# Another order of a forward attention segment, with V's turns taken off TensorE and a two-halves out-projection

## The chip, the core and the metric

The kernel runs on one core of one Trainium2 chip. The metric is the time of one execution on the device in microseconds: before the change 3229.96 us, the median of three runs from 3228.64 to 3230.3.

## What is computed

A transformer block with adaptive layer norms, forward and backward: an attention with a recurrent memory, then a gated feed-forward layer, then all gradients. The change is in the forward attention. Cut to that part, the reference is:

```python
mem = mem0                                  # 8 rows of 512
for s in range(64):                         # segments of 32 rows
    h = concat([mem, x[s * 32:(s + 1) * 32]])       # 40 rows
    q, k, v = h @ Wq, h @ Wk, h @ Wv                # 32 heads of 128
    p = softmax(where(mask, q @ k.T * scale, -1e9))
    o = (p @ v) @ Wo                                # over all heads: 40 rows of 512
    mem = o[:8]                                     # the next segment's memory
    outs.append(o[8:])
```

All inputs and outputs are bf16. The eight rows of memory make the segments strictly sequential: the projections of a segment need the first eight output rows of the one before.

## The kernel before, in words

`phase2` holds the forward attention: a Python loop over 64 segments that is unrolled into one instruction stream, in the order in which it is written. At its end the stream from the loop's start on is pinned (`pin`), so that each engine works through it in program order. Tiles have a fixed number of buffers; a write to a buffer waits for the reads of what it held.

**A and B rows.** Of the 40 rows of a segment, 8 are memory and 32 are input. The memory rows and the first 24 input rows are the 32 "A" rows, projected in the loop itself (`proj`, through `col_pass` at L222). The last eight input rows of four segments, 32 rows together, are projected in one "B" pass per Q, K and V ahead of time (`proj_b`). A pass is in two halves; each half is 16 matmuls of 512 columns, four of which lie side by side in four groups of 32 array columns, into one PSUM tile `pass_ps` [128, 512]. Partition group j holds rows 0 to 31 for a quarter of the heads. ScalarE or VectorE copies the half into row tiles `RA` or `RB`.

**The heads.** Eleven groups of three heads (the last of two) hold 120 rows each. For the first eight groups the three heads lie in partition groups 0 to 2; the heads of the last three groups come from partition group 3 of the row tiles, "far" pieces in what follows.

**Turning.** `turn_half` turns half a row tile by four TensorE transposes (L231); `to_heads` copies the result into `qT`, `kT` and `vT` (the tiles of `XT`), columns by group: one copy for the first eight groups, then one or two for the far ones. For A rows this is done in the loop for K, Q and V. For B rows a turned batch `b_cols` lies ready, from which GpSimd copies eight columns a head into the tiles (`tails_in`, L65).

**V in rows.** PV needs V in rows, `Vst` [128, 11 x 128]. GpSimd copies its first eight groups from `RA` (L715, L717), GpSimd-issued DMAs fill the tail rows 96 to 119 of these groups from `RBv` (`v_tails`, L624: three a segment), and the last three groups come back from `vT` by three TensorE transposes (`vst(2)`, L680).

**A segment**, in the order of its TensorE instructions:

1. the projections V, K, Q; meanwhile K and Q rows go to DRAM for the backward (`rows_out`, L554 and L555, issued by SyncE)
2. the turns: first halves of K and Q, both of V, second halves of K and Q; `vT` is stored whole to DRAM (L738)
3. `st_exp`: scores in three blocks of four, four and three groups, two matmuls a group (one adds the mask), then exp on ScalarE into `ET`
4. `den` and `pv` for each block: row sums by a matmul with ones, their reciprocal, PV into `or_ps`, and O scaled into `Ost` by one VectorE instruction (L694); SyncE issues a transposing DMA of `ET` into `Pst` (L748), for the backward
5. `ott`: O turned by TensorE transposes into `OT`; `Ost` and `OT` are stored (L771, L779)
6. `outproj`: 32 matmuls of 512 columns (`col_mm`, L211), one a head, four side by side, into `at_ps` [128, 512]; so four partial sums lie in four partition groups
7. `fold_split`: the partial sums as two bf16 parts each (hi by ScalarE, L278; the rest, lo, by VectorE, L282), in two halves of 256 columns
8. the slot "f2": a B pass of V, K or Q in the first three segments of four (both halves), the tail rows' out-projection in the fourth
9. `fold_sum`: eight matmuls (L291) with a selection matrix add the partial sums and turn the result; ScalarE copies its first eight columns into the next segment's `hT` (L785)

At the start of the next segment GpSimd normalizes the turned P of the last (`norm`, L792) and SyncE stores it (L794). GpSimd's order between two segments is: row store (L306), `v_tails`, `tails_in` for K, V and Q, `tail.collect` (L1822), the input part of `hT` (L511), the normalization, the two copies into `Vst`. In SyncE's: transpose of P, stores of O and O turned, B rows where there are any, store of P, K and Q rows.

In sixteen of the segments eight more matmuls and a weight load of the modulation (`mod_rest`) ride along, and a layer norm of later input rows (`p1`) is spread over each four segments.

The backward reads V turned once a segment, from the DRAM tile `VT`, as the moving operand of dO V (L1416).

Of the kernel before, what the change touches and what calls it, by code (L numbers as in the profile page):

```python
# [40 lines left out]
class K:  # L41
# [43 lines left out]
    def alloc_dram(self):  # L85
# [8 lines left out]
        self.VT = d("VT", [NS, 128, cfg.XW], BF16)  # L94
# [20 lines left out]
    def phase0(self):  # L115
# [10 lines left out]
        nc.vector.tensor_tensor(self.foldsel[:], fs2[:, 0, :], fs2[:, 1, :], op=ALU.add)  # L126
        self.later = []
# [80 lines left out]
    def col_mm(self, ps, lhsT, w, n, total):  # L208

        j = n % 4  # L210
        self.nc.tensor.matmul(ps[32 * j:32 * j + 32, :], lhsT=lhsT, rhs=w, start=(n < 4), stop=(n >= total - 4),  # L211
                              tile_position=(0, 32 * j))

# [190 lines left out]
    def phase2(self):  # L404
        nc, tc, cfg, io = self.nc, self.tc, self.cfg, self.io
        D, DC, H, E, L, M, T, G, NS = cfg.D, cfg.DC, cfg.H, cfg.E, cfg.L, cfg.M, cfg.T, cfg.G, cfg.NS
        GW = 128
# [10 lines left out]
        with ExitStack() as ctx:  # L418
# [26 lines left out]
            XT = {x: ptiles(x + "T", 1, w=cfg.XW)[0] for x in "qkv"}  # L445
# [26 lines left out]
            with tc.tile_pool(name="p0", bufs=1) as p0:  # L472
# [21 lines left out]
                for f in zeros:  # L494
                    f()
                self.load_heads(p0, Wv, io["A_Wv"])
                self.load_heads(p0, Wk, io["A_Wk"])
                p1(1, 0)
                self.load_heads(p0, Wq, io["A_Wq"])
# [38 lines left out]
            def to_heads(eng, xt, src, i0, n, r0, w, o):  # L538
# [4 lines left out]
                d = xt[:, 120 * i0:120 * (i0 + n)].rearrange("p (i x) -> p i x", x=120)[:, :, b:b + 3 * w]  # L543
                self.evac(eng, d.rearrange("p i (j r) -> p i j r", r=w), s4[:, :, 0:3, o:o + w])
# [23 lines left out]
            def b_pieces(t):  # L568
# [4 lines left out]
                def proj_b(x, hf):  # L573
                    hb = hxs[t][1]
                    pass_half(x, hf, lambda c: hb[:, c, :, :].rearrange("p s q -> p (s q)"), RBt[x], ("act", "dve")[hf])
                    if hf == 1 and x != "v":
                        rows_out(RBt[x], DR[x], t * nseg_t, nseg_t)

                def turn_b(x):
# [3 lines left out]
                    def f():  # L583
# [7 lines left out]
                return {(0, "f2"): [P("v", 0), P("v", 1)], (1, "f2"): [P("k", 0), P("k", 1)], (1, "turn"): [T_("v")],  # L591
                        (2, "f2"): [P("q", 0), P("q", 1)], (2, "turn"): [T_("k")], (3, "turn"): [T_("q")]}
# [8 lines left out]
            q_first = first.pop((2, "f2")) + first.pop((3, "turn")) + [evac_turned]  # L601
            for fs in first.values():
                for f in fs:
                    f()
            evac_turned()
# [8 lines left out]
            tail = TailRows(self, sb2, psp, psb, 1, "ao", self.AOB, 1)  # L614

            def tails_in(xs, s):
                for x in xs:
                    to_heads("pool", XT[x], btails[s // nseg_t][x][:], 0, 8, 32, 8, 8 * (s % nseg_t))

            def v_tails(s):  # L620

                for j in range(3):
                    o = 32 * j + 8 * (s % nseg_t)
                    nc.gpsimd.dma_start(Vst[96 + 8 * j:104 + 8 * j, 0:1024], RBv[(s // nseg_t) % 2][o:o + 8, 0:1024])  # L624

            v_tails(0)
            tails_in("vk", 0)
            i0 = len(self.traced())
            for s in range(NS):
# [6 lines left out]
                QT, KT, VT = XT["q"], XT["k"], XT["v"]  # L636
# [12 lines left out]
                def turn(x, hf, eng):  # L649
                    tp = turn_half(RA[x], hf)  # L650
                    to_heads(eng, XT[x], tp[:], 4 * hf, 4, 0, 32, 0)
# [13 lines left out]
                def den(pi):  # L665
# [7 lines left out]
                    nc.vector.reciprocal(rden[:, pi * PG:pi * PG + n], den_ps[0][0:120, pi * PG:pi * PG + n])  # L673
# [9 lines left out]
                def vst(pi):  # L683
                    ps, n = transposes_part(VT, pi, 120)
                    self.evac("act" if pi == 2 else "dve", part3(Vst, pi)[:, 0:n, :], ps)

                def pv(pi):
                    or_ps = ps_f32("or_ps")
                    n = min(PG, G - pi * PG)
                    for j in range(n):  # L690
                        g = pi * PG + j
                        nc.tensor.matmul(or_ps[:, j, :], lhsT=ET[:, g * GW:(g + 1) * GW], rhs=Vst[:, g * GW:(g + 1) * GW],  # L692
                                         start=True, stop=True)
                    nc.vector.tensor_tensor(part3(Ost, pi)[0:120, 0:n, :], or_ps[0:120, 0:n, :],  # L694
                                            rden[:, pi * PG:pi * PG + n].unsqueeze(2).to_broadcast([120, n, 128]), op=ALU.mult)

                def ott(pi):
                    ps, n = transposes_part(Ost, pi)
                    self.evac("dve" if pi == 2 else "act", part3(OT, pi)[:, 0:n, :], ps)

                at_ps = [None]
                n_at = [0]

                def outproj(h0, h1):
                    if at_ps[0] is None:
                        at_ps[0] = psp.tile([128, 512], F32, name="at_ps", tag="p")
                    for h in range(h0, h1):
                        off = (h // 3) * GW + (h % 3) * 32
                        self.col_mm(at_ps[0], OT[:, off:off + 32], Wo[:, h, :], n_at[0], H)
                        n_at[0] += 1  # L710
# [3 lines left out]
                proj("v", 0, "act")  # L714
                nc.gpsimd.tensor_copy(Vst[0:96, 0:512], RA["v"][0:96, 0:512])  # L715
                proj("v", 1, "dve")
                nc.gpsimd.tensor_copy(Vst[0:96, 512:1024], RA["v"][0:96, 512:1024])  # L717
                if s == NS - 1:
# [3 lines left out]
                if 1 <= s4 <= 3:  # L722
                    p1(s // nseg_t + P1_AHEAD, s4)
                proj("k", 0, "act")
                proj("k", 1, "dve")
                proj("q", 0, "dve")
                proj("q", 1, "act")
                if s == 0:
                    for f in q_first:
                        f()  # L730
                    tails_in("q", 0)
                turn("k", 0, "dve")
# [1222 lines left out]
```

## Time and profile before

| | |
|---|---|
| span of the profiled execution | 3233.1 us |
| TensorE (PE) busy | 2984.2 us, 92% |
| VectorE (DVE) busy | 1589.7 us, 49% |
| ScalarE (ACT) busy | 1200.4 us, 37% |
| GpSimd (POOL) busy | 1430.5 us, 44% |
| first and last copy into hT, 63 in all | 60.5 and 1042.3 us |
| transposing DMA of ET, time of its issue on SyncE | 1274 / 1407 / 2342 ns (least, median, most) |
| normalization of P on GpSimd | 2530 ns, 63 times |
| V tail DMA, issue on GpSimd | 511 ns median, 192 times |
| V tail DMA, issue to landing | 1.9 / 3.7 / 6.3 us |

How to read it: busy time counts an instruction from its start to its end, and matmuls overlap each other, so a high share of TensorE doesn't say by itself that it never waits. In timelines, the bracket at the end of a line gives the time in which the engine stood idle before it and what released it. "SPq" is the queue that SyncE issues DMAs from. PEld is the load of a stationary operand. Relative to the whole, the forward segments take about 1000 of 3230 us.

### The profile page before, as it was taken

What the parts mean: (1) busy time and instruction counts of PE and PEld (TensorE: products, weight loads), DVE (VectorE), ACT (ScalarE), POOL (GpSimd) and SP (SyncE); (2) the same over time, 40 slices, a digit from 0 to 9 for tenths busy, and PEclk for the clock granted to TensorE, in tenths of its full rate; (3) what the DMA queues carried; (4) which work ended last, traced back from release to release, by engine and by line L of the source; (5) the groups of instructions that cost most, each with busy time, mean ns of one, the idle gap of its engine ahead of it and who ended that gap; (6) DMA issues with size and microseconds to landing.
All of it is one profiled execution on the core that took longest, in us unless ns stands there. A gap on an engine that the chain in (4) does not pass through costs nothing.

```text
span 3233.1 us, 96019 instructions
## 1 busy us (share of the span) xinstructions
PE 2984.2 (92%) x38574; PEld 1709.9 (53%) x38650; DVE 1589.7 (49%) x4170; ACT 1200.4 (37%) x2842; POOL 1430.5 (44%) x3037
## 2 busy tenths in 40 slices
PE   6999999999998799988989999999999969999999
PEld 3555555555555444444555555555555534455454
DVE  5655555655555777642245545555554531322321
ACT  3555555555554333322134444444444420100111
POOL 3555555565555465630144444444444431333322
PEclk8999999999999899998999999999999989999999
DMA  8565555555555788896679999999999999898986
GB/s 295 174 173 169 171 169 172 165 172 173 162 164 174 220 212 210 211 260 217 219 199 263 265 247 273 261 261 259 258 272 258 261 233 219 241 209 198 202 231 159
DMA packets 862018, 699.40 MB, mean 216 GB/s; under 512 B 560690, under 2 KB 734274, under 8 KB 861444
## 3 DMA queue, kind: packets, MB, share of 16 engines
q1 hardware_dynamic: 737220, 483.44, 62.8%
q0 software_dynamic: 52912, 147.43, 13.4%
q10 hardware_dynamic: 71440, 62.40, 7.6%
q8 instruction: 304, 4.98, 0.7%
q14 instruction: 142, 1.16, 0.1%
HBM read 293.60 MB, written 275.02 MB: 176 GB/s over the span
## 4 chain that ended last, share of the span: by engine, by line
PE 43%; DMA 8%; ACT 2%; issue 2%; DVE 1%; SPq 1%; POOL 1%; ACTq 0%; DVEq 0%; POOLq 0%
PE dh_ps L211 9%; PE gps L1748 9%; PE pass_ps L222 4%; PE g_ps L1437 4%; PE gps L1146 3%; PE gps5o L1761 3%; PE dh_tps L211 2%; DMA rows<-DKR 2%; PE tps L1352 2%; PE dp_ps L1416 1%; DMA rows<-OSR 1%; PE dp_ps L1424 1%; ACT RAd L61 1%; PE dh_ft L291 1%; PE turn_ps L1318 1%
## 5 line engine op out<-in xcount | busy, mean ns | idle before, releaser
L1748 PE MATMUL gps<-rows,hrows 128*128 128x512 bf16 (+2 forms) x2124 | 415.8, 355 | 3.8 <-ACT ot L61 1.9
L1748 PEld LDWEIGHTS <-hrows 128*128 128x128 bf16 x2160 | 211.3, 98 | 206.6 <-issue 2.6
L222 PEld LDWEIGHTS <-hT 128*32 128x32 bf16 x6144 | 158.4, 97 | 177.9 <-ACT hT L785 24.5
L1466 POOL COPY dOst<-RAd 96x512 bf16<-96x512 bf16 x128 | 78.2, 612 | 355.9 <-DVE RAd L63 339.8
L1752 POOL DMA_DIRECT2D out_dram<-ot x108 | 81.2, 753 | 231.4 <-DVE ot L63 135.4
L63 DVE CAST ot<-gps 128x512 bf16<-128x512 f32 (+3 forms) x76 | 47.8, 632 | 247.8 <-DMA out_dram<-ot 99.1
L792 POOL TENSOR_TENSOR Pst<-Pst,rden 120x1408 bf16<-120x1408 bf16 x63 | 159.4, 2531 | 15.1 <-issue 7.1
L282 DVE TENSOR_TENSOR dh_lo<-dh_ps,dh_hi 128x256 bf16<-128x256 f32 x128 | 48.4, 420 | 239.1 <-ACT dh_hi L278 239.1
L1761 PE MATMUL gps5o<-WoT,rows 128*128 128x512 bf16 x588 | 131.6, 382 | 27.8 <-DMA rows<-OSR 27.2
L306 POOL DMA_DIRECT2D AOA<-at_rb x64 | 36.7, 574 | 250.8 <-DVE at_rb L305 137.3
L61 ACT ACTIVATE ot<-gps 128x512 bf16<-128x512 f32 (+3 forms) x75 | 41.0, 547 | 284.4 <-PE gps L1748 103.1
L222 PE MATMUL pass_ps<-Wv,hT 128*32 128x512 bf16 x2048 | 122.3, 380 | 18.1 <-ACT hT L785 18.1
L694 DVE TENSOR_TENSOR Ost<-or_ps,rden 120x512 bf16<-120x512 f32 (+1 forms) x192 | 124.3, 647 | 23.0 <-PE or_ps L692 0.8
L211 PE MATMUL dh_ps<-WvT,dVT 128*32 128x512 bf16 x2048 | 134.5, 381 | 0.2 <-issue 0.2
L1426 DVE SCALAR_TENSOR_TENSOR dS<-dp_ps,Pst_l 128x512 bf16<-128x512 f32 (+1 forms) x192 | 112.2, 640 | 35.3 <-PE dp_ps L1424 35.3
L222 PE MATMUL pass_ps<-WoT,dyT 128*32 128x512 bf16 x2048 | 121.9, 380 | 5.2 <-ACT dyT L1525 5.2
L211 PE MATMUL at_ps<-Wo,OT 128*32 128x512 bf16 x2048 | 123.3, 383 | 0.0
L211 PE MATMUL dh_ps<-WkT,dKT 128*32 128x512 bf16 x2048 | 122.6, 380 | 0.7 <-issue 0.7
L211 PE MATMUL dh_ps<-WqT,dQT 128*32 128x512 bf16 x2048 | 122.0, 379 | 0.0
L222 PE MATMUL pass_ps<-Wq,hT 128*32 128x512 bf16 x2048 | 121.6, 379 | 0.0
L222 PE MATMUL pass_ps<-Wk,hT 128*32 128x512 bf16 x2048 | 121.6, 379 | 0.0
L61 ACT ACTIVATE dVT<-g_ps 128x512 bf16<-128x512 f32 (+1 forms) x192 | 107.8, 562 | 35.9 <-PE g_ps L1437 20.0
(410 smaller groups left out, 7135.2 us busy)
## 6 DMA issues: line engine op xcount, KB each, us to landing
OSR<-Ost SPq DMA_DIRECT2D x64, 352.0 KB
OT<-OT SPq DMA_DIRECT2D x64, 352.0 KB
PS<-Pst SPq DMA_DIRECT2D x64, 352.0 KB
OT_l<-OT SPq DMA_DIRECT2D x64, 352.0 KB
Pst_l<-PS SPq DMA_DIRECT2D x64, 352.0 KB
DKR<-rows_x POOLq DMA_DIRECT2D x64, 352.0 KB, 6.0
DVR<-rows_x POOLq DMA_DIRECT2D x64, 352.0 KB, 7.5
DQR<-rows_x POOLq DMA_DIRECT2D x64, 352.0 KB, 6.1
```

The source lines that it names most:

```text
L61: return nc.scalar.activation(out, in_, AF.Copy)
L211: self.nc.tensor.matmul(ps[32 * j:32 * j + 32, :], lhsT=lhsT, rhs=w, start=(n < 4), stop=(n >= total - 4), tile_position=(0, 32 * j))
L222: self.nc.tensor.matmul(ps[32 * j:32 * j + 32, :], lhsT=lhs(c), rhs=rhs, start=(c == 0), stop=(c == DC - 1), tile_position=(0, 32 * j))
L694: nc.vector.tensor_tensor(part3(Ost, pi)[0:120, 0:n, :], or_ps[0:120, 0:n, :], rden[:, pi * PG:pi * PG + n].unsqueeze(2).to_broadcast([120 ...
L792: nc.gpsimd.tensor_tensor(Pst[0:120, :, :], Pst[0:120, :, :], rden[:, :].unsqueeze(2).to_broadcast([120, G, 128]), op=ALU.mult)
L1146: nc.tensor.matmul(ps[:], lhsT=h2r[:, j, c * 128:(c + 1) * 128], rhs=xr[:, j, :], start=(j == 0), stop=(j == NT - 1))
L1426: nc.vector.scalar_tensor_tensor(out=part3(dS, pi), in0=ps[:, 0:n, :], scalar=cfg.scale, in1=part3(Pst, pi), op0=ALU.mult, op1=ALU.mult)
L1437: nc.tensor.matmul(ps[:, j, :], lhsT=lh[:, g * GW:(g + 1) * GW], rhs=rh[:, g * GW:(g + 1) * GW], start=True, stop=True)
L1466: nc.gpsimd.tensor_copy(dOst[0:96, 512 * hf:512 * hf + 512], RAd[0:96, 512 * hf:512 * hf + 512])
L1748: nc.tensor.matmul(ps[:, 0:ng * E], lhsT=hrows[:, tp_, c * 128:(c + 1) * 128], rhs=rows[:, tp_, 0:ng * E], start=(tp_ == 0), stop=(tp_ == ...
L1752: nc.gpsimd.dma_start(outw[c * 128:(c + 1) * 128, h0:h0 + 3 * (ng - 1) + 1:3, :], ot[:, 0:ng * E].rearrange("p (h e) -> p h e", e=E))
L1761: nc.tensor.matmul(pss[gg][:], lhsT=rows[:, tp_, gg * E:(gg + 1) * E], rhs=dyrows[:, tp_, :], start=(tp_ == order[0]), stop=(tp_ == order[ ...
```

## The change

What it does, part by part:

- **Order.** The projections come in the order K, Q, first half of V, then all turns, then the second half of V. The weights are loaded in that order too. Each turn is copied in two steps, the first eight groups of all four halves, then the far pieces; first halves by ScalarE, second halves by VectorE.
- **V not turned on TensorE.** `vT` is gone, with its turns, tails and transposes. The last three groups of `Vst` come from `vshift`, three matmuls that move partition group 3 of `RA` to groups 0 to 2, and one VectorE copy; their tail rows by three more DMAs in `v_tails`. The turned V for the backward comes from a transposing DMA of `Vst` into `VTr`, issued by SyncE ahead of that of `ET`; its store follows in the next segment, with that of P. `VT` in DRAM gets 128 in place of 120 columns a group.
- **O scaled by two engines.** Blocks 0 and 2 by VectorE, block 1 by ScalarE as four copies with a scale for each partition. One reciprocal covers blocks 0 and 1. The O transposes follow all three blocks.
- **Out-projection of 256 columns a matmul.** `pair_mm`: two heads share four column groups, each head once with the left and once with the right 256 columns of `Wo`. So `at_ps` is [128, 256], with two partial sums for each half; one hi and one lo part remain (`split_pair`), and `sum_pair` folds with a selection of two groups.
- **The slots.** B passes are halved: "f1" before the fold, "f2" behind the copy into `hT`; so is the tail's out-projection.

The diff, cut to its core:

```diff
-        self.VT = d("VT", [NS, 128, cfg.XW], BF16)
+        self.VT = d("VT", GL, BF16)
...
+    def pair_mm(self, ps, x, w, n, total):
+        nc = self.nc
+        for j in range(4):
+            d, k = j // 2, j % 2
+            nc.tensor.matmul(ps[32 * j:32 * j + 32, :], lhsT=x[k], rhs=w[k][:, 256 * d:256 * d + 256], start=(n == 0),
+                             stop=(n == total - 1), tile_position=(0, 32 * j))
+
+    def split_pair(self, pool, ps, name):
+        nc = self.nc
+        hi = pool.tile([128, 256], BF16, name=name + "_hi", tag="hi0", bufs=1)
+        nc.scalar.activation(hi[:], ps[:], AF.Copy)
+        lo = pool.tile([128, 256], BF16, name=name + "_lo", tag="lo0", bufs=1)
+        nc.vector.tensor_tensor(lo[:], ps[:], hi[:], op=ALU.subtract)
+        return hi, lo
...
             def v_tails(s):
...
                 for j in range(3):
-                    o = 32 * j + 8 * (s % nseg_t)
-                    nc.gpsimd.dma_start(Vst[96 + 8 * j:104 + 8 * j, 0:1024], RBv[(s // nseg_t) % 2][o:o + 8, 0:1024])
+                    nc.gpsimd.dma_start(Vst[96 + 8 * j:104 + 8 * j, 0:1024], rb[32 * j + o:32 * j + o + 8, 0:1024])
+                    nc.gpsimd.dma_start(Vst[96 + 8 * j:104 + 8 * j, 1024:1408], rb[96 + o:104 + o, 384 * j:384 * j + 384])
...
+                def turns():
+                    tps = []
+                    for x in "kq":
+                        for hf in range(2):
+                            tps.append((x, hf, ("act", "dve")[hf], turn_half(RA[x], hf)))
+                            to_heads(tps[-1][2], XT[x], tps[-1][3][:], 4 * hf, 4, 32, 0, far=False)
+                    for x, hf, eng, tp in tps:
+                        to_heads(eng, XT[x], tp[:], 4 * hf, 4, 32, 0, own=False)
...
+                def vshift():
+                    sh = ps_f32("sh_ps")
+                    shf = sh[:].rearrange("p g x -> p (g x)")
+                    for hl in range(3):
+                        nc.tensor.matmul(shf[32 * hl:32 * hl + 32, 0:384], lhsT=self.ident[96:128, 96:128],
+                                         rhs=RA["v"][96:128, 384 * hl:384 * hl + 384], start=True, stop=True,
+                                         tile_position=(96, 32 * hl))
+                    nc.vector.tensor_copy(Vst[0:96, 1024:1408], shf[0:96, 0:384])
...
-                proj("v", 0, "act")
+                proj("k", 0, "dve")
+                proj("k", 1, "act")
...
+                proj("q", 0, "dve")
+                proj("q", 1, "act")
...
+                proj("v", 0, "dve")
                 nc.gpsimd.tensor_copy(Vst[0:96, 0:512], RA["v"][0:96, 0:512])
+                turns()
                 proj("v", 1, "dve")
                 nc.gpsimd.tensor_copy(Vst[0:96, 512:1024], RA["v"][0:96, 512:1024])
...
                 st_exp(0)
                 st_exp(1)
-                vst(2)
+                vshift()
+                st_exp(2)
+                if s < NS - 1:
+                    nc.sync.dma_start(VTr[:], Vst[:, :], transpose=True)
                 den(0)
-                pv(0)
-                st_exp(2)
+                or0 = pv(0)
...
                 den(1)
-                pv(1)
+                recip(0, 2)
+                or1 = pv(1)
+                ost(0, or0, "dve")
+                ost(1, or1, "act")
+                den(2)
+                or2 = pv(2)
+                recip(2, 3)
+                ost(2, or2, "dve")
                 fill(s4, "turn")
...
-                outproj(0, H)
+                at_ps = outproj()
                 evac_turned()
                 if s + 1 < NS:
                     v_tails(s + 1)
-                    tails_in("kvq", s + 1)
-                parts = self.fold_split(sb2, at_ps[0], "at")
+                    tails_in("kq", s + 1)
+                parts = self.split_pair(sb2, at_ps, "at")
                 tail.collect(s4, [OT])
                 nc.sync.dma_start(self.OT[s], gl3(OT))
-                fill(s4, "f2")
+                fill(s4, "f1")
...
+                ft = self.sum_pair(psp, parts, "at", "p")
+                if hT_next is not None:
+                    nc.scalar.activation(hT_next[:, :, 0:M], ft[:, :, 0:M], AF.Copy)
+                fill(s4, "f2")
...
                 def norm(s=s, Pst=Pst, rden=rden):
...
+                    nc.sync.dma_start(self.VT[s], VTr[:])
                     nc.sync.dma_start(self.PS[s], Pst[:])
```

After the last segment, whose V is not transposed by a DMA, three blocks of TensorE transposes and ScalarE copies make its `VTr`.

## The prediction, made before the changed kernel ran

> **What bounds the kernel now.** I read the page's busy table first, then busy time by stretch, the TensorE timeline of one forward segment, the waits, and last the timelines of the DMA-issuing queue (SPq) and of GpSimd. The change touches the forward attention loop; the attention backward only reads V in another layout. The stretch that holds the loop (columns: stretch, length, busy time and count of PE, PEld, DVE, ACT, POOL, then clock, DMA share, GB/s):
>
> ```profile
> 40.00:1060.00 1020.00, 946.94 (x16672) 589.60 (x16668) 603.65 (x1903) 518.63 (x1306) 585.49 (x1412) 1.00 0.59 172
> ```
>
> The loop is a third of the run, at full clock. 63 copies into hT (L785), one per segment, start from 60.5 to 1042.3 us: (1042.3 - 60.5) / 62 = 15.84 us a segment (about 16.25 in the sixteen segments that also do modulation products, 15.7 in the rest). PE is 93% busy, but matmul durations overlap, so I count from starts. One segment runs from 650.34 to 665.95, 15.61 us. Its TensorE timeline (start, duration, instruction, count, idle before it and releaser):
>
> ```profile
> 657.47 0.22 PE L659 MATMUL st_ps<-maskT,ident 128*128 128x120 bf16 x1
> 657.87 0.23 PE L657 MATMUL st_ps<-qT,kT 128*128 128x120 bf16 x1 [0.18 <-DVE qT L63]
> ...
> 660.70 0.40 PE L680 MATMUL tps<-ident,Ost 128*128 128x128 bf16 x4
> 661.45 0.34 PE L680 MATMUL tps<-ident,Ost 128*128 128x128 bf16 x3 [0.35 <-DVE Ost L694]
> 661.73 1.91 PE L211 MATMUL at_ps<-Wo,OT 128*32 128x512 bf16 x32
> 663.46 1.90 PE L222 MATMUL pass_ps<-Wq,hb 128*32 128x512 bf16 x32
> 665.29 0.19 PE L291 MATMUL at_ft<-foldsel,at_hi 128*128 128x32 bf16 x1
> ...
> 665.95 0.83 PE L222 MATMUL pass_ps<-Wv,hT 128*32 128x512 bf16 x12 [0.29 <-ACT hT L785]
> ```
>
> A 32-matmul pass takes 663.46 - 661.73 = 1.73 us of issue. Where a start comes later than its predecessor's share, TensorE stood still: 0.35 us before the second score block (Q columns not copied), 0.27, 0.53 and 0.12 around the O transposes (VectorE scales all of O), 0.10 before the fold, 0.44 before the next segment (fold, then hT), and 0.11 before the turns: 1.92 us, so 13.7 us of work. The loop is bound by TensorE's work plus the round trip through it.
>
> Two helpers have slack now. SPq and GpSimd in the same segment:
>
> ```profile
> 659.94 2.18 SPq L748 DMA_TRANSPOSE Pst<-ET  x1
> 662.22 0.53 SPq L771 DMA_DIRECT2D OSR<-Ost  x1
> ...
> 670.07 0.39 SPq L794 DMA_DIRECT2D PS<-Pst  x1
> 670.56 0.36 SPq L554 DMA_DIRECT2D KST<-RA1k  x1
> ```
>
> ```profile
> 659.98 1.51 POOL L624 DMA_DIRECT2D Vst<-RBv  x3 [0.96 <-PE or_ps L692]
> 661.49 0.76 POOL L65 COPY kT<-b_colsk 128x192 bf16<-128x192 bf16 x4
> 662.19 0.76 POOL L65 COPY vT<-b_colsv 128x192 bf16<-128x192 bf16 x4
> 662.90 0.76 POOL L65 COPY qT<-b_colsq 128x192 bf16<-128x192 bf16 x4
> 663.61 0.40 POOL L1822 COPY ao_tail<-OT 128x264 bf16<-128x264 bf16 x1
> 663.96 0.26 POOL L511 COPY hT<-hx 128x96 bf16<-128x96 bf16 x1
> 665.15 2.53 POOL L792 TENSOR_TENSOR Pst<-Pst,rden 120x1408 bf16<-120x1408 bf16 x1 [0.93 <-DMA Pst<-ET]
> ```
>
> The transpose issued at 659.94 released GpSimd's normalization at 665.15: 5.2 us. Other segments give 4.4 (no wait, so an upper bound) to 6.3 us. SPq works in order: the store of P waits for that normalization, the K and Q rows queue behind the store.
>
> **What the skill says.** "TensorE: Matmul & The Clock Gate", section "Wait — 56ns, not 53.3ns?", says that starts of matmuls never come closer than about 25 ns, however few columns; here the eight 32-column fold matmuls start 25 to 40 ns apart, which agrees. "TensorEngine Tiling (Array Packing)", "Restrictions", says that column tiling disables fast weight load: the out-projection is column-tiled, and at 646.12 its first sixteen weight loads stand within 0.55 us, (0.55 - 0.10) / 15 = 30 ns apart, which is what a load costs when no matmul holds it back. "Advanced Engine Details and Errata", "X-Bar Transpose (TRN2)", calls transposing DMAs as fast as regular ones. This trace disagrees: from 661.0 to 663.0 the DMA share is 0.52, 2.71, 0.65, 0.37 over half-microsecond windows, some 2.1 us of all engines, for 352 KB, while the stores of O and of O turned then took about 2.3 us for 704 KB, at 290 to 428 GB/s: half the time per byte. I use the trace.
>
> **The change part by part**, per segment on TensorE.
>
> V off TensorE: removed are eight turns (0.44 us), three transposes back (0.17) and a quarter of a 0.45 us batch turn (0.11). Added are three 32-row matmuls of 384 columns (vshift): 0.16 us side by side, 0.48 one after another; I take 0.2. Net -0.5.
>
> Out-projection: 64 matmuls of 256 columns for 32 of 512. By columns it stays at 1.73 us (27 ns each); at the 30 ns of the weight loads it is 1.92; if nothing overlaps better than today's 54 ns it is 3.46. I take 1.92: +0.2. The split becomes one hi (0.38) and one lo (0.42) in place of two of each (0.66 and 0.76 here).
>
> Order: the second V half (0.87 us) stands between the turns and the scores and covers the Q copies, so the 0.35 goes. Its own evacuation queues on VectorE behind four copies of turned columns and is done some 0.7 us after it; the sixteen matmuls of score blocks 0 and 1 take 0.86, and the copies delay the evacuation by up to 0.3: vshift waits 0.2, with score block 2 behind it on TensorE.
>
> O by two engines: block 0 on VectorE (0.69), block 1 as four ScalarE copies (about 0.25 each: hT takes 0.197 for 32 columns, at_hi 0.381 for 256), block 2 on VectorE (0.56). But the reciprocal now covers blocks 0 and 1 at once, so block 0 can't be scaled before the second denominators. Counted from the segment's start: V's second half ends at 6.07 and is evacuated from 6.36 to 7.05; vshift starts at 7.1, score block 2 ends at 7.58, denominators and PV 0 and 1 fill TensorE to 8.32, with the reciprocal from 8.35 to 8.50, and the last ones to 8.6. Block 0 of O is scaled at 9.2, so the first O transpose starts at 9.25: 0.65 of wait, 0.2 where a batch turn (0.45) stands before it, 0.4 in the mean. ScalarE ends block 1 near 9.5, VectorE block 2 at 9.8, so the other transposes wait 0.17 together; OT's first block is copied at 10.2, 0.17 more before the out-projection. 0.74 against 0.92 before.
>
> Half a batch pass (0.87) before the fold, half behind it: at_ps to fold is 0.25 + 0.38 + 0.02 + 0.42 + 0.06 = 1.13, so 0.26 of wait; the second half hides the 0.44 of the hT copy.
>
> Sum: three projections 5.19, turns 0.88, scores 1.18, vshift 0.2, denominators and PV 0.97, batch turns 0.22, O transposes 0.6, row turns 0.07, out-projection 1.92, batch passes 1.73, fold 0.2 = 13.16; waits 0.2 + 0.74 + 0.26 = 1.2. TensorE alone would run at 14.4 us.
>
> The new helper loop is what I think binds. V turned for the backward now comes from a second transposing DMA that reads Vst whole. Before the next tail rows go into Vst (six GpSimd DMAs now) it must have landed. Behind those on GpSimd, in order, stand the K and Q tails, the collecting copy, hT, then the normalization; behind that on SPq the P store and four row stores, and behind those the next V transpose. The cycle: issue to landing 5.0 (4.4 to 6.3); six DMA issues at 0.513 = 3.08; two tails at 0.71 = 1.42; collect 0.35; hT 0.23; normalization 2.53; hand-offs 0.1; five SPq issues 2.2 (1.95 to 2.4 by segments nearby). Sum 14.9 us, from 14.1 to 16.4. TensorE meets it at PV, which needs the Vst copies behind the normalization; it has about 1.9 us of lead, used up in a few segments, and then keeps the helpers' pace.
>
> Costed at nothing: the VT store moving behind the normalization's issue (SPq waits there anyway); VT rows of 2816 in place of 2656 bytes in the backward (20 KB in 1.7 MB of loads a segment); RA and tail copies of V that go (GpSimd had slack), except that they shorten the cycle above.
>
> Ends: in the first segment K and Q weights come first, V later, and scores can start while V loads: about 3 us less before the scores at 49.5. After the last segment eleven transposes and three copies: 2 us more.
>
> **The rivals.**
> *TensorE bound*: the transpose lands in 4.4 and the rows issue in 1.95, the cycle falls to 14.1 and TensorE's 14.4 rules, 14.5 with modulation. For it: transposes that were not waited for. Against: today's transpose has an idle DMA ring, the new one has 880 KB of P and K/Q rows issued just ahead. 62 x 1.34 = 83 less, and the ends: 3146.
> *Transpose contention*: two transposes and the rows slow each other, landing 6.3 or more, cycle 16.4: 62 x 0.56 = 35 more, 3264, slower. For it: the 2.71 share window; DMA share would be (0.59 x 15.84 + 2.1) / 15 = 0.76. Against: most landings are near 5.
> *256-column matmuls do not overlap* (54 ns): TensorE 15.9 plus modulation, 16.0: 62 x 0.16 = 10 more, less the ends: about 3238. For it: weight loads double. Against: 30 ns seen.
>
> **How the numbers follow.** Helper loop 0.60, TensorE bound 0.20, contention 0.12, no overlap 0.08. The likeliest: 62 x (15.84 - 14.95) = 55 less, 14.95 being 14.9 with a little for segments that miss each other; -3 and +2 at the ends: 3230 - 56 = 3174. The range takes in both of the first cases: down to 3136 (TensorE at 14.25), up to 3228 (cycle at 15.8). Faster: 0.60 + 0.20; the no-overlap case is split between same and slower.
>
> **What would show it.** The hT copies 14.9 to 15.0 us apart; GpSimd idle before the V tail DMAs until the DMA VTr<-Vst; VTr's issue straight behind the Q rows; PE idle before or_ps until GpSimd's Vst copy; 64 at_ps matmuls in 1.7 to 1.95 us. A period near 14.4 with VTr waiting for vshift's copy would say TensorE binds; a landing above 6 us, contention. I am wrong altogether if some wait that I hide (the first O transpose, vshift) is above 1 us.

## The result and the profile after

The changed kernel takes 3287.26 us (median, 3283.25 to 3290.1), the one before 3230.13 us beside it: a ratio of 1.0177, 95% interval 1.0159 to 1.0194. It is slower by 57 us. I had predicted 3174, with a range up to 3228.

Where the time went, from the two traces (spans 3281.5 and 3233.1 us, 48.4 apart): the 63 copies into hT start from 62.8 to 1083.4 us, against 60.5 to 1042.3. That is 41.0 us more in the forward loop, of which 62 intervals of 16.46 in place of 15.84 us make 38.7 and a later first copy 2.3. This mean interval between two copies into hT is called the period below. From the last hT copy to the first use of dOT in the backward it is 605.5 in place of 599.0 us, 6.5 more. The rest of the backward is level within 1 us.

Busy time by stretch, the kernel after (columns as in the prediction: busy PE, PEld, DVE, ACT, POOL with counts, clock, DMA share, GB/s):

```profile
40.00:1060.00 1020.00, 938.28 (x17448) 608.82 (x17448) 546.65 (x1450) 460.75 (x1246) 607.96 (x1306) 0.96 0.76 188
```

TensorE is about as busy as before in the same stretch (938 against 947 us), but gets through fewer segments in it (1020 / 16.46 = 62.0 against 64.4), and its mean clock has fallen from 1.00 to 0.96. DMA is busier, 0.76 against 0.59. The TensorE timeline of one segment shows what it waits for:

```profile
685.85 1.93 PE L220 MATMUL at_ps<-Wo,OT 128*32 128x256 bf16 x64
687.60 1.04 PE L249 MATMUL pass_ps<-Wq,hb 128*32 128x512 bf16 x16
...
689.93 1.90 PE L249 MATMUL pass_ps<-Wk,hT 128*32 128x512 bf16 x32
...
695.35 1.05 PE L249 MATMUL pass_ps<-Wv,hT 128*32 128x512 bf16 x16
...
697.27 0.34 PE L723 MATMUL sh_ps<-RA0v,ident 32*32 32x384 bf16 x3
...
697.87 0.24 PE L704 MATMUL dc_ps<-ones,ET 128*128 128x1 bf16 x4
700.00 0.38 PE L733 MATMUL or_ps<-Vst,ET 128*128 128x128 bf16 x4 [1.89 <-POOL Vst L776]
```

The new parts cost what they should: 64 out-projection matmuls in 687.60 - 685.85 = 1.75 us, and no gap before the turns, before the second score block or around hT. One new wait undoes it: PV stands 1.89 us for GpSimd's copy of V into `Vst`. Before PV the idle time that this copy ends is 56.6 us, in 43 segments. Why GpSimd is late, its own timeline shows, with that of SyncE's queue (SPq) in the same segment:

```profile
691.22 0.51 POOL L653 DMA_DIRECT2D Vst<-RBv  x1 [3.94 <-PE pass_ps L249]
...
694.23 0.76 POOL L65 COPY kT<-b_colsk 128x192 bf16<-128x192 bf16 x4
...
696.23 2.53 POOL L851 TENSOR_TENSOR Pst<-Pst,rden 120x1408 bf16<-120x1408 bf16 x1
...
699.32 0.62 POOL L776 COPY Vst<-RA0v 96x512 bf16<-96x512 bf16 x1
```

```profile
685.45 1.47 SPq L793 DMA_TRANSPOSE VTr<-Vst  x1
687.03 2.93 SPq L798 DMA_TRANSPOSE Pst<-ET  x1
...
698.79 0.33 SPq L854 DMA_DIRECT2D PS<-Pst  x1
...
700.18 1.05 SPq L585 DMA_DIRECT2D QST<-RA1q  x1
701.28 0.68 SPq L586 DMA_DIRECT2D QST<-RA1q  x1
702.31 2.05 SPq L793 DMA_TRANSPOSE VTr<-Vst  x1
```

Read it as a ring. V is transposed from 685.45; its tail rows may go into `Vst` only when that has landed, at 691.22, 5.77 us later; six DMA issues and the tails of K and Q follow on GpSimd, then the normalization (696.23), which releases the store of P on SPq (698.79); four row stores, and the next V transpose at 702.31. One turn of 16.86 us. The turns last 14.6 to 20.2 us, 16.47 in the mean; in the three longest GpSimd pauses for another 2.9 us between two tail DMAs, and I don't know why. The bracket of the first GpSimd line names a projection that ended at 690.1, a microsecond too early to be what released it. In other segments it names the transfer itself, for instance at 643.56:

```profile
643.56 0.52 POOL L653 DMA_DIRECT2D Vst<-RBv  x1 [1.31 <-DMA VTr<-Vst]
```

GpSimd stands idle ahead of these DMAs in all 62 turns of the ring. And the V transpose never waits for its data: in every turn it starts 0.33 to 0.72 us after the issue ahead of it on SPq ends, and the last copy into `Vst` has ended 0.46 us before it or more. So the ring is closed in every turn without TensorE, and TensorE follows it. Its four legs, from start to start, means over 62 turns, beside what I had predicted (they add up to a turn by construction; what they show is where the time is):

| leg | predicted | measured |
|---|---|---|
| V transpose issued, to first tail DMA | 5.0 (4.4 to 6.3) | 5.64 (4.24 to 6.86) |
| tail DMAs, K and Q tails, collect, hT, to the normalization | 5.18 | 5.20 |
| normalization, to the store of P | 2.53 | 2.56 |
| store of P, to the next V transpose | 2.2 (1.95 to 2.4) | 3.07 (2.73 to 4.36) |
| sum | 14.9 | 16.47 |

The second leg is about 5.0 us in most turns; the three with the pause, at 7.9, lift its mean. The ring I described is there, and binds; two of its legs are longer than I had them, by 0.64 and 0.87 us. Those 1.5 us turn a gain of 0.9 us a segment into a loss of 0.6.

### The profile page after: what moved, and what is told of

It reads as the page before. It is cut to its first block, busy times and chain, and to the rows that moved or that the text cites. A ratio compares the mean times of both kernels' runs of the same rounds, so it can differ in the third digit from the quotient of the medians.

```text
span 3281.5 us, 98764 instructions
## 1 busy us (share of the span) xinstructions
PE 3020.3 (92%) x40069; PEld 1756.2 (54%) x40069; DVE 1550.0 (47%) x3769; ACT 1160.6 (35%) x2829; POOL 1478.0 (45%) x2973
## 3 DMA queue, kind: packets, MB, share of 16 engines
q8 instruction: 316, 5.18, 0.7%
## 4 chain that ended last, share of the span: by engine, by line
PE 39%; DMA 8%; issue 5%; ACT 2%; POOL 1%; DVE 1%; SPq 1%; ACTq 0%; POOLq 0%; DVEq 0%
PE dh_ps L212 9%; PE gps L1812 5%; PE pass_ps L249 4%; PE g_ps L1501 3%; PE gps5o L1825 3%; PE gps L1210 3%; PE dh_tps L212 2%; DMA rows<-DKR 2%; PE tps L1416 2%; DMA rows<-OSR 1%; PE dp_ps L1480 1%; PE dp_ps L1488 1%; ACT RAd L61 1%; PE dh_ft L318 1%; PE turn_ps L1382 1%
## 5 line engine op out<-in xcount | busy, mean ns | idle before, releaser
L653 POOL DMA_DIRECT2D Vst<-RBv x192 | 97.8, 509 | 210.9 <-PE pass_ps L249 122.9
L309 DVE TENSOR_TENSOR dh_lo<-dh_ps,dh_hi 128x256 bf16<-128x256 f32 x128 | 48.4, 420 | 239.1 <-ACT dh_hi L305 239.1
L220 PE MATMUL at_ps<-Wo,OT 128*32 128x256 bf16 x4096 | 138.7, 294 | 0.4
L249 PE MATMUL pass_ps<-Wv,hT 128*32 128x512 bf16 x2048 | 133.3, 380 | 0.0
L63 DVE CAST RA0v<-pass_ps 128x512 bf16<-128x512 f32 x128 | 88.5, 692 | 88.9 <-PE pass_ps L249 62.0
L733 PE MATMUL or_ps<-Vst,ET 128*128 128x128 bf16 x704 | 71.7, 228 | 62.9 <-POOL Vst L776 56.6
L61 ACT ACTIVATE dVT<-g_ps 128x512 bf16<-128x512 f32 (+1 forms) x192 | 107.8, 561 | 40.6 <-PE g_ps L1501 22.3
```

The lines of the kernel that those rows point to most:

```text
L61: return nc.scalar.activation(out, in_, AF.Copy)
L63: return nc.vector.tensor_copy(out, in_)
L220: nc.tensor.matmul(ps[32 * j:32 * j + 32, :], lhsT=x[k], rhs=w[k][:, 256 * d:256 * d + 256], start=(n == 0), stop=(n == total - 1), tile_p ...
L249: self.nc.tensor.matmul(ps[32 * j:32 * j + 32, :], lhsT=lhs(c), rhs=rhs, start=(c == 0), stop=(c == DC - 1), tile_position=(0, 32 * j))
L653: nc.gpsimd.dma_start(Vst[96 + 8 * j:104 + 8 * j, 0:1024], rb[32 * j + o:32 * j + o + 8, 0:1024])
```

## The experiments

The theory now (H) is the ring through the single buffer of `Vst`: a longer leg costs its length in every segment, and where a second buffer opens the ring, TensorE binds again. Its rivals: the second transposing DMA slows the first or TensorE's helpers by its traffic (contention), whoever waits for it; or the loss lies in the other parts, the order, the halves of the B passes, the 256 columns or the scaling. All ratios below are against the kernel before, run beside it.

### The ring opened: two buffers of Vst

```diff
-            Vst = ptiles("Vst", 1)[0]
+            Vsts = ptiles("Vst", 2)
...
+                Vst = Vsts[s % 2]
```

(and the same choice in `v_tails`).

> The changed kernel with two buffers for Vst, used in turn, so that the tail DMAs of the next segment no longer wait for the landing of the V transpose; nothing is left out and the V transpose still moves the same bytes. Theory H (the helper cycle V transpose, tail DMAs, normalization, P store, row stores sets the pace): the cycle is cut, TensorE's own 14.4 to 14.8 us a segment rules, (16.46 - 14.6) x 62 = 115 us less than the changed kernel: about 3172, and TensorE no longer waits for Vst before or_ps. Theory C (two transposing DMAs and the rows overload the DMA engines): what is moved is unchanged, so the period stays above 16 us: 3260 to 3290. Theory T (TensorE's own new work or its lower clock): no change, 3287.

Measured: 3209.02 us, 0.9932 (0.9912 to 0.9952), a period of 15.23 us. The wait before PV is gone (1.9 us in 4 segments, after 56.6 in 43). One buffer is thus what costs 78 us between this kernel and the changed one. The DMA engines are busier than in the changed kernel (0.80 against 0.76 of the time), since the same transfers fall into shorter segments, and yet the loop is faster:

```profile
40.00:1060.00 1020.00, 959.49 (x18276) 621.65 (x18265) 620.13 (x1546) 485.82 (x1305) 647.58 (x1364) 0.99 0.80 205
```

But TensorE doesn't reach my 14.4 either. One new wait is plain in the TensorE timeline:

```profile
713.89 0.62 PE L258 MATMUL turn_ps<-ident,RA1k 128*128 128x128 bf16 x8
715.52 0.62 PE L258 MATMUL turn_ps<-ident,RA1q 128*128 128x128 bf16 x8 [1.01 <-DVE RA1q L63]
```

In some segments the layer norm of later input rows has its scale step on VectorE ahead of the copy of Q: 14.1 us of idle time before the turns, in 12 segments. I take it up below.

### The transfer taken away

```diff
+            zeros.append(lambda: nc.gpsimd.memset(VTr[:], 0.0))
...
-                if s < NS - 1:
-                    nc.sync.dma_start(VTr[:], Vst[:, :], transpose=True)
```

> The changed kernel without the V transposing DMA in the 63 segments: VTr is zero once and its store goes on, so the backward reads zeros for V in all segments but the last (that part of the computation is left out). Theory H: as the kernel with two buffers for Vst, 3160 to 3175; the transfer itself costs nothing once nothing waits for it. Theory C: clearly faster than the kernel with two buffers, by 1 us a segment or more (60 us). Theory T: no change from 3287.

Measured: 3215.32 us, 0.9959 (0.9947 to 0.9971), period 15.29. With no V transpose at all the loop is no faster than with one that nothing waits for (15.23), though the DMA engines are busy for 0.62 in place of 0.80 of the time (40 to 1000 us). So the transfer's traffic by itself costs nothing that can be seen here; the loss comes from its being waited for. This is where traffic that slows the loop whoever waits for it falls as the cause. That one transfer delays another inside the ring is a different matter, taken up below.

### Row stores taken out of the ring

```diff
                 if s < NS - 1:
                     nc.sync.dma_start(VTr[:], Vst[:, :], transpose=True)
+                if stores:
+                    stores.pop()()
...
-                    nc.sync.dma_start(self.PS[s], Pst[:])
+                    stores.append(lambda: nc.sync.dma_start(self.PS[s], Pst[:]))
```

The store of P, which waits for the normalization, goes behind the next V transpose on SPq.

> The changed kernel with the store of the normalized P issued behind the V transpose of the next segment instead of ahead of the K and Q rows; nothing is left out. Theory H: the 3.07 us from the P store to the V transpose leave the cycle, in their place stand the two copies into Vst, some 1.3 us: 16.46 - 1.7 = 14.8 us a segment, about 3180. Theory C or T: no change, 3287.

Measured: 3256.99 us, 1.009 (1.0058 to 1.0122). The profiled execution, the longest of five at 3275.07 us, has a period of 16.04. Faster than the changed kernel by 30 us, so the SPq leg did count, but far from the 3180 I expected. SPq's queue and GpSimd's timeline show a second ring that I had made (first the view of SPq's waits from 200 to 1000 us: total, times, longest):

```profile
SPq L801 <- DMA PS<-Pst: 146.4, 50, 4.5
```

```profile
652.48 2.53 POOL L854 TENSOR_TENSOR Pst<-Pst,rden 120x1408 bf16<-120x1408 bf16 x1 [3.09 <-DMA Pst<-ET]
```

`Pst` has one buffer too. The store of P now leaves late, the transpose of P waits for it in all 50 segments of this stretch, and the normalization waits for that. It isn't a clean removal of a leg, but it shows the same thing a second time: here too a single buffer that a DMA reads closes a ring.

### A leg made longer

```diff
-                if s < NS - 1:
-                    nc.sync.dma_start(VTr[:], Vst[:, :], transpose=True)
...
                     nc.sync.dma_start(Pst[:], ET[:, :], transpose=True)
+                    nc.sync.dma_start(VTr[:], Vst[:, :], transpose=True)
```

> The changed kernel with the two transposing DMAs in the other order: P first, V behind it; nothing is left out. Theory H: V's landing comes one transpose later (1.65 us of issue between them), the cycle grows by about 1.65 to 18.1 us a segment: 3287 + 100 = about 3390. Theory C: the same bytes in the same time, 3287. Theory T: 3287.

Measured: 3384.33 us, 1.0489 (1.0465 to 1.0513), period 17.90. The leg from the P store to the V transpose is 4.83 in place of 3.07 us, the one to the first tail DMA 5.36 in place of 5.64: 1.48 us more, and the period is 1.44 longer. The bytes are the same as in the changed kernel. The ring passes what is put into it on to the whole loop, nearly one for one.

### What the neighbour adds to the landing

```diff
-                    nc.sync.dma_start(Pst[:], ET[:, :], transpose=True)
+                    pass
```

(`Pst` is a tile of zeros instead.)

> The changed kernel without the P transposing DMA: P stays zero for the backward in all segments but the last (that part is left out); the normalization runs on zeros at its usual cost. It measures V's landing alone. If the P transpose issued 1.6 us behind V's slows V's [...], the landing falls from 5.64 us to 4.4 to 4.8, the cycle to about 15.4, and the run to 3215 to 3230. If V's landing is slow by itself, or by the rows ahead of it, 5.6 stays and so does 3287.

Measured once: 3261.44 us, period 16.09. From V's issue to the first tail DMA it is now 5.10 us, with the transpose of P behind it 5.64 (means over 62 turns, each uncertain by about 0.1). So about 0.5 us of the landing comes from the transpose that follows; the other 5.1 remain without it. I had expected 4.4 to 4.8, so most of what my landing lacked is this neighbour.

### V's part alone, and the rest alone

On the kernel before, only V taken off TensorE, with the ring, in the old order:

```diff
+                    nc.gpsimd.dma_start(Vst[96 + 8 * j:104 + 8 * j, 1024:1408], rb[96 + o:104 + o, 384 * j:384 * j + 384])
...
-                turn("v", 0, "act")
-                turn("v", 1, "act")
+                vshift()
...
-                nc.sync.dma_start(self.VT[s], VT[:, :])
+                if s < NS - 1:
+                    nc.sync.dma_start(VTr[:], Vst[:, :], transpose=True)
```

> The kernel before with this one part of the change alone: V off TensorE (three shifting matmuls after the first turns, V turned by a transposing DMA where the V store stood, six tail DMAs); order V, K, Q, scaling on VectorE, 512-column out-projection and whole batch passes as before. Nothing is left out. Theory H: the same helper cycle as in the changed kernel, 16.3 to 16.5 us a segment, 3230 + 0.55 x 62 + 6 for the end = about 3270. Rival P: with its 0.5 us less of TensorE work it is faster than before, 3200 to 3225.

Measured: 3315.7 us, 1.0248 (1.0213 to 1.0283), period 16.92, more than I expected. Its legs are 5.16, 5.16, 2.90 and 3.57 us, 16.79 in sum. So in the old order this part loses 84 us by itself, and the other parts win some of it back. But not all of the 84 is shown to be the ring's. GpSimd stands idle ahead of the tail DMAs in 50 of 62 turns, not in all, and TensorE waits only 3.4 us before PV. It waits for VectorE's copies of Q and K instead: 29.2 us before their turns and 26.4 before the scores, against 0 and 9.1 in the kernel before (40 to 1060 us).

On the kernel before, only the 256-column out-projection and the halved B passes:

```diff
-                outproj(0, H)
+                at_ps = outproj()
...
-                parts = self.fold_split(sb2, at_ps[0], "at")
+                parts = self.split_pair(sb2, at_ps, "at")
...
+                fill(s4, "f1")
...
                 fill(s4, "f2")
```

> The kernel before with one other part of the change alone: the out-projection of 256 columns, its single hi and lo part, and the batch passes in two halves before and behind the copy into hT. Nothing is left out. If the parts that don't touch V are gains, the waits before the fold and before the next segment (0.10 + 0.44) shrink to 0.1 to 0.26: 0.3 to 0.4 us a segment, 3205 to 3213. Rival (256-column matmuls cost TensorE as much as they save): 3225 to 3240.

Measured: 3223.06 us, 0.9969 (0.996 to 0.9978), period 15.68. A gain, and where it was expected: the idle time before the projections falls from 18.1 to 1.2 us. But it is 9 us where I expected 19 to 27. What takes back the rest in the old order I did not settle.

Putting V back on TensorE in the changed kernel, turned behind the second score block, was meant as the opposite test:

```diff
-                vshift()
+                turn_v()
                 st_exp(2)
-                if s < NS - 1:
-                    nc.sync.dma_start(VTr[:], Vst[:, :], transpose=True)
+                vst(2)
```

> The changed kernel with one part undone: V is turned on TensorE again (behind score block 1, with its tails, its three transposes back and its old layout in the backward); order of Q and K, scaling by two engines and 256-column out-projection stay. Nothing is left out. Theory H: without the V transposing DMA no helper cycle binds; TensorE has 0.44 + 0.17 + 0.11 - 0.2 = 0.5 us more than with two Vst buffers (15.23), about 15.7 us a segment, 3225 to 3245. Rival P (another part of the change is what costs): still above 3270.

Measured: 3274.27 us, 1.0121 (1.0084 to 1.0158), period 16.39. I placed the turns where nothing covers their copies. TensorE's timeline:

```profile
731.76 0.33 PE L723 MATMUL tps<-ident,vT 128*128 128x128 bf16 x3 [0.65 <-ACT vT L61]
```

Idle time before transposes is 47.5 us, before turns 20.7 (40 to 1060 us). The run replaced one wait by two others; it is inconclusive for H.

### The layer norm moved too, and two parts taken back out

With two buffers of `Vst`, the pieces of the layer norm go to the end of the segment, behind the row store, where VectorE is free:

```diff
-                if 1 <= s4 <= 3:
-                    p1(s // nseg_t + P1_AHEAD, s4)
...
+                if s4 <= 2:
+                    p1(s // nseg_t + P1_AHEAD, s4 + 1)
```

> Two Vst buffers as in the first experiment, and the layer norm pieces of later rows (statistics, scale, shift) at the end of the first three segments of four instead of between the K and Q passes of the last three. Nothing is left out. In the kernel with two buffers TensorE stood 1 us before Q's turns where VectorE was at the scale step (s4 = 2 and 3 take 15.05 and 15.37 us against 14.8). If that is the cause, 0.2 us a segment less: 3209 - 13 = 3196. If it is not, 3209.

Measured: 3190.17 us, 0.9867 (0.9838 to 0.9897): faster than the kernel before by 42 us and than the changed one by 97. Its period is 14.99 us, 14.8 in segments without modulation. A segment on TensorE, from one K projection to the next:

```profile
728.62 1.90 PE L249 MATMUL pass_ps<-Wk,hT 128*32 128x512 bf16 x32
...
736.56 0.24 PE L705 MATMUL dc_ps<-ones,ET 128*128 128x1 bf16 x4
736.66 0.38 PE L734 MATMUL or_ps<-Vst,ET 128*128 128x128 bf16 x4
...
738.15 1.09 PE L717 MATMUL tps<-ident,Ost 128*128 128x128 bf16 x11 [0.29 <-DVE Ost L746]
...
739.28 1.93 PE L220 MATMUL at_ps<-Wo,OT 128*32 128x256 bf16 x64
...
743.37 0.61 PE L249 MATMUL pass_ps<-Wk,hT 128*32 128x512 bf16 x8
```

PV follows the denominators without a gap, and the clock is back at full (40 to 1000 us):

```profile
40.00:1000.00 960.00, 931.31 (x17903) 601.72 (x17902) 563.17 (x1489) 470.30 (x1280) 626.05 (x1344) 1.00 0.82 206
```

From this kernel two parts of the change were taken back, one at a time (the kernel before ran in 3231.90 us beside the first and 3231.89 us beside these two, so their times can be set side by side). Out-projection with 512 columns and a fold in two hi and two lo parts:

```diff
-                    ps = psp.tile([128, 256], F32, name="at_ps", tag="p")
+                    ps = psp.tile([128, 512], F32, name="at_ps", tag="p")
...
-                parts = self.split_pair(sb2, at_ps, "at")
+                parts = self.fold_split(sb2, at_ps, "at")
```

> The fastest kernel so far (two Vst buffers, layer norm pieces late) with the out-projection of 512 columns and two hi and two lo parts again. Nothing is left out. hi and lo take 0.66 + 0.76 in place of 0.38 + 0.42, with 0.87 of batch pass in front of the fold: 0.5 us a segment of wait before the fold, 3190 + 31 = 3221. If 256 columns bring nothing: 3190.

Measured: 3225.18 us, 0.9981 (0.997 to 0.9991), period 15.45. Idle time before the fold is 22.3 us in 68 places, against 3.8 in 10. The 256 columns with their shorter fold are worth 35 us here, of which this idle time explains about half.

The middle block of O scaled by VectorE:

```diff
-                ost(1, or1, "act")
+                ost(1, or1, "dve")
```

> The fastest kernel so far with the middle block of O scaled by VectorE instead of ScalarE. Nothing is left out. VectorE's last block is ready 0.69 later, so the last O transpose and what stands behind it wait up to 0.7: 3190 + 62 x 0.6 = 3227. If the two-engine scaling brings nothing because the wait for the first block dominates: 3190.

Measured: 3228.04 us, 0.999 (0.9978 to 1.0003), period 15.48. Idle time before O's transposes is 41.7 us in 145 places, against 9.7 in 33. The two engines are worth 38 us here.

These worths can't be read as shares of the gain: together they are 73 us, where the whole kernel gains 42 on the kernel before, and the 256 columns with the halved passes gained only 9 in the old order. Whether the two overlap or the rest of the change loses the difference, the runs don't say.

## Why the prediction was wrong

**The bound was named rightly.** "The new helper loop is what I think binds" held: GpSimd is idle before the V tail DMAs, PE is idle before PV, and the V transpose stands straight behind the Q rows without a wait of its own. The run with a longer leg confirms it, and the second buffer opens it.

**The step that failed is the sum of the cycle.** Two terms of it were too small.

- *"five SPq issues 2.2 (1.95 to 2.4)"*: it measured 3.07. I had added up durations of issues. Measured from the start of the P store to the start of the V transpose, the leg is never under 2.73 us. In the turn that ends at 685.45 the five issues last 0.33 + 0.36 + 0.43 + 0.57 + 0.43 = 2.12 us, as predicted, but the leg is 685.45 - 682.66 = 2.79: 0.32 lies between the issues and 0.35 between the last row store and the transpose. In other turns a store of Q rows takes 1 us to issue, as at 700.18.
- *"issue to landing 5.0"*: it measured 5.64. I took it from the transpose of P in the kernel before, which had no transpose close behind it. The new one has. Without that neighbour it is 5.10, with it 5.64.

The other two legs came within 0.03 us in the mean, the tail leg with some luck: most turns take 5.0 where I had 5.18, and three long ones make up for it. My bounds for the cycle, 14.1 to 16.4, nearly hold the 16.47, but the forecast's upper end stood at a cycle of 15.8, since I gave "transpose contention" only 0.12. That rival's 16.4 is close to the measured period, but not for its reason: it wanted a landing of 6.3 or more, and the larger error is in the SPq leg. Half a microsecond of contention is real; added to my 14.9 it gives about 15.45, under the 15.84 of the kernel before, so by itself it would have left the change ahead.

**The second error is TensorE's own 14.4**, which set how much the other end could bring. With the ring open and the layer norm out of the way it is 14.8 in plain segments. In the segment shown, from the K projection to the denominators it takes 7.94 us, where the terms of my sum give 5.19 + 0.88 + 1.18 + 0.2 + 0.2 = 7.65; from there to the out-projection 2.72 for 2.60; from there to the next segment 4.09 for 4.11. So 0.3 of it lies in projections, turns and scores, which I took without the tenth or so lost from one kind of matmul to the next. I had also overlooked the layer norm's step on VectorE in front of Q's copy; in the old order the V projection stands ahead of that step. With the ring open the kernel took 3209 us, and 3190 with the layer norm moved as well, not 3146.

**What came as predicted.** The 64 matmuls of 256 columns took 1.75 us (I took 1.92, the floor by columns was 1.73), so "256-column matmuls do not overlap" fell. The Trainium skill ("TensorEngine Tiling (Array Packing)", "Restrictions") says that column tiling disables fast weight load; that does not show as a cost here, at 27 ns a matmul. My 1.92 rested on a misreading: of the sixteen weight loads at 646.12 in the kernel before, the first eight start 3 to 5 ns apart and the rest in fours every 0.21 us, the pace of the matmuls, so 30 ns is a mean and not what a load costs. `vshift` took 0.27 for my 0.2, and no wait of its own. In the changed kernel at_ps to the next stage, fold and hT, behaves as said: 0.22 us in the fold, ahead of its lo part, for my 0.26, and nothing before K's projection.

That the DMA share came out at 0.76, as I gave it for the contention case, is luck. I had divided by a period of 15; with the measured 16.46 the same sum gives 0.70. The change added 0.76 x 16.46 - 0.59 x 15.84 = 3.2 us of all engines a segment, where I had 2.1.

**The ends.** I expected -3 and +2 us, and got +2.3 and +6.5. In the first segment the scores start at 49.29 instead of 49.47: the B passes of Q, K and V all still stand ahead of them. Then PV waits 3.63 us for tail rows that are sent only after V's pass. In the last segment the scores wait 1.31 us for GpSimd's tails of Q and PV 2.07 us for its copy of V: the ring is late there too, and nothing after it makes it up. The out-projection then takes 3.27 in place of 1.75 us, at the lower clock.

## What to carry to other kernels

A buffer that a DMA reads and that is then refilled closes a ring through every queue between the two; time a leg of that ring from start to start, gaps included, since durations of issues alone came out over a quarter short here. When the ring's sum lies close to the present period (here 14.9 against 15.84), ask first whether a second buffer opens it: here that alone was 78 us. And where a transfer is judged by an older one of the same kind, look at what is queued right behind each.

## What the runs showed of the hardware

- A transposing DMA with another behind it in the same queue was waited for 0.54 us longer (5.64 against 5.10 us). The Trainium skill ("Advanced Engine Details and Errata", "X-Bar Transpose (TRN2)") calls them as fast as regular ones. That differs here. An estimate from DMA share times period: one transpose of 352 KB took 2.7 us of all engines (V's: 0.80 x 15.23 with it and two buffers, 0.62 x 15.29 without it) or 2.9 (P's: 0.76 x 16.46 with it, 0.60 x 16.09 without), where the kernel before moved 704 KB in plain stores in about 2.3. The issue differs too: 1.47 and 2.05 us for the V transposes shown above, 0.33 us for the plain store of P, which moves as many bytes.
- In the changed kernel TensorE lost clock around long waits, and after them too. Two neighbouring stretches, in one of the three turns with the pause on GpSimd:

```profile
824.00:832.00 8.00, 3.97 (x55) 2.67 (x53) 2.56 (x9) 2.97 (x9) 7.30 (x17) 0.77 0.20 69
832.00:840.00 8.00, 7.56 (x122) 6.31 (x121) 2.82 (x9) 3.21 (x8) 1.80 (x5) 0.59 1.03 216
```

In the first TensorE is busy for 4 of 8 us; in the second it has its work back and runs it at 0.59 of the clock, the out-projection in 839.27 - 836.48 = 2.79 us:

```profile
836.48 2.95 PE L220 MATMUL at_ps<-Wo,OT 128*32 128x256 bf16 x64
```

Not every wait costs clock. Split 200 to 1000 us into a hundred windows of 8 us. In the changed kernel TensorE waits 54.4 us there in 59 waits, the longest 2.76, and the clock is below 0.95 in 17 windows. With V back on TensorE it waits as much, 53.6 us, but in 86 waits of at most 1.36, and no window is below 0.95. With two buffers the longest is 1.69, and again none is; with P transposed first it is 3.05, and 43 are. Where between 1.69 and 2.76 us the difference sets in, and whether length alone decides it, these runs don't show. Inside the loop the ring sets the pace and holds no work of TensorE, so the lower clock can add little there; how little was not measured. In the last segment it adds the 1.5 us above.
